# Attention, expert MLP and soft mixture on one core: scores on four array tiles, dummy products near the end, and a new order

## The chip, the cores and the metric

The kernel runs on one core of one Trainium2 chip. The metric is the device time of one execution in microseconds (us). The profile and the traces come from one further execution, recorded by the hardware profiler.

## The reference

Three stages follow each other. Everything is float32.

```
# 4 batches x 8 heads x 768 steps, head size 40: a gated recurrence
m_new  = max(f + m, i);  f' = exp(f + m - m_new);  i' = exp(i - m_new)
C = f' C + i' v k^T;     n = f' n + i' k
y = sigmoid(o) * (C q) / max(|n.q|, 1)
# y -> x: 3072 tokens x 320
h = x @ w_in (320 x 2048);  x = (h * sigmoid(h)) @ w_out (2048 x 320)
# soft mixture: 8 experts, 4 slots each
logits = x @ phi (320 x 32)
slot_in = softmax over tokens(logits)^T @ x
slot_out[e] = relu(slot_in[e] @ w1[e] (320 x 1024)) @ w2[e] (1024 x 320)
out = softmax over slots(logits) @ slot_out
```

## The kernel before, in words

**Attention** goes in 24 tiles of 128 steps (4 batches of 6), each with all 8 heads as 4 pairs. For a tile n, `load_qk` and `load_v` bring queries, keys and values; `mask`, `arg` and `exp` make the decay factors (`exp` on ACT, L566); `sc` multiplies keys with queries, per head and per half of 64 steps (L597); `sw` multiplies the scores with the factors (DVE, L604); `st` makes the state update (L629) and `sadd` adds it; `pv` takes scores and state to the values (L655); `xT` transposes the result and splits it into a high and a low part.

**The MLP** goes in 12 blocks of 256 tokens. `mlp.b.q` is one of 8 chunks of block b: 16 products of 128x256 (L702) and the activation (ACT, L704). `gU` transposes the activated rows (DVE, L711). `w_out` is not multiplied token by token: `wpT` and `wp` (L450 to L475) form `w_out @ phi` once, `lg` uses it for the logits of a block (L721), `lsum` and `slots` keep the running softmax and the weighted sums over tokens (L731, L745, L749, L762, L765). Before `wp`, each of the 16 pieces of `w_out` is loaded (L423) into one of five `cv` buffers and turned from its stored form into float32 by three operations, on ACT, DVE and DVE (L372, L374, L376).

**The end** begins after `slots.11`, the last block's sums: `slot_in` (L863, L873, L885), the experts' first layer `s1` (L905), its transposes (L915), the second layer `s2` in two column halves of 152 and 168 (L932), and `out` (L950), which multiplies with the softmax over slots and stores. The expert weights are loaded by `load_w1` and `load_w2` (L838 to L845). The 32 pieces of `w2` lie in memory that belongs to the MLP's buffers until these are done.

**What sets the order.** `ORDER` is a list of tokens written out by hand; a token such as `sc.7` runs the function `op_sc` for tile 7 to its next `yield`. The list's order is the order on each engine. The table `ENG` says for some operations whether DVE (V), ACT (A) or GpSimd (G, called POOL in the profile) does them. SP issues all DMAs, in order, with 8 in flight: each waits for the one eight before it.

**PSUM.** The accumulator memory is used through three tags, `h`, `t` and `w`, with two buffers each. A `w` buffer has two banks. Before the change `sc` writes into a `t` buffer of one bank, and `st` and `pv` write into a `w` buffer; `slots` takes both `w` buffers.

In the score product of the old kernel a head that lies on the upper 64 rows of the array writes to the upper 64 columns, and one on the lower rows to the lower columns: `tile_position=(o, o)`. `pv` uses all four combinations of row and column half, with a bank for each row half: `tile_position=(o, 64 * ch)`.

Of the kernel before, what the change touches and what calls it, by code (L numbers as in the profile page):

```python
# [1033 lines left out]
```

## Time and profile before

| what | value |
|---|---|
| time, median of 3 runs (range) | 458.77 us (457.52 to 459.79) |
| the profiled execution: time, span | 461.74 us, 459.8 us |
| granted TensorE clock, mean | 0.962 |
| busy: PE, weight loads, DVE, ACT, POOL | 408.9, 332.2, 268.8, 257.8, 114.5 us |
| share of the chain that ended last: PE, DMA, ACT, DVE | 50%, 16%, 13%, 12% |
| moved by DMA | 72.31 MB |

PE is TensorE's matrix products, PEld its weight loads, which run beside them. A granted clock of 1.0 is 2.4 GHz and 0.5 is 1.2 GHz. The chain is followed back from the last instruction, at each step to what released it. In a table of stretches each row has the length of the stretch, the busy time of each engine with the number of instructions, the clock, the mean busy share of the DMA engines (it can pass 1 for short stretches), and the transfer rate. In a timeline a row is a run of like instructions: start, duration, engine, line, and in brackets the idle time before it and what ended it.

### The profile page before, as it was taken

How to read it: one execution, taken by the hardware profiler on the slowest of the kernel's cores; microseconds unless marked ns; L12 is line 12 of the kernel's file. 1: busy time of each engine (PE TensorE's matmuls, PEld its weight loads, DVE VectorE, ACT ScalarE, POOL GpSimd, SP SyncE). 2: the span in 40 equal slices, each digit the busy share in tenths (PEclk: the TensorE clock that was granted, in tenths of full speed). 3: DMA queues.
4: the chain of work that ended last, by engine and by line, in shares of the span. 5: the costliest groups of instructions: out<-in, count | busy, mean ns of one | idle time of the engine just before them, and what ended most of it. 6: DMA issues, size and time to landing. Idle time of an engine off the chain costs nothing.

```text
span 459.8 us, 15017 instructions
## 1 busy us (share of the span) xinstructions
PE 408.9 (89%) x6458; PEld 332.2 (72%) x6458; DVE 268.8 (58%) x637; ACT 257.8 (56%) x473; POOL 114.5 (25%) x155
## 2 busy tenths in 40 slices
...
DMA packets 59218, 73.27 MB, mean 159 GB/s; under 512 B 4976, under 2 KB 46640, under 8 KB 59152
## 3 DMA queue, kind: packets, MB, share of 16 engines
q1 hardware_dynamic: 59152, 72.31, 53.9%
q8 instruction: 51, 0.84, 0.8%
q14 instruction: 15, 0.12, 0.1%
...
## 4 chain that ended last, share of the span: by engine, by line
PE 50%; DMA 16%; ACT 13%; DVE 12%; issue 4%; SPq 2%; POOL 1%; ACTq 0%; DVEq 0%; POOLq 0%
PE h L702 26%; DMA w<-in_moe_w 7%; PE w L655 4%; PE t L721 4%; PE w L762 3%; PE t L597 3%; DMA mb<-md 3%; ACT L704 3%; PE w L629 2%; DMA cv<-in_moe_w_out 2%; DMA rawi<-in_moe_w_in 2%; ACT gT L704 2%; ACT L745 2%; DMA vb<-in_vh 1%; PE t L675 1%
## 5 line engine op out<-in xcount | busy, mean ns | idle before, releaser
L702 PE MATMUL h<-xh,wh 128*128 128x256 f32 x384 | 85.7, 305 | 8.4 <-ACT gT L704 8.3
L704 ACT ACTIVATE gT<-h 128x512 f32<-128x512 f32 x96 | 55.5, 597 | 55.0 <-PE h L702 54.4
L702 PEld LDWEIGHTS h<-xh,wh 128*128 128x128 f32 x384 | 60.1, 193 | 25.4 <-ACT gT L704 17.6
L702 PE MATMUL h<-xl,wh 128*128 128x256 f32 x384 | 78.2, 286 | 0.0
L702 PE MATMUL h<-xh,wl 128*128 128x256 f32 x384 | 78.1, 285 | 0.0
L711 DVE STREAM_TRANSPOSE g<-gT 128x512 f32<-128x512 f32 x96 | 62.6, 685 | 3.0 <-ACT gT L704 2.8
L702 PEld LDWEIGHTS h<-xl,wh 128*128 128x128 f32 x384 | 60.4, 193 | 0.2 <-DVE xl L683 0.2
L702 PEld LDWEIGHTS h<-xh,wl 128*128 128x128 f32 x384 | 60.5, 194 | 0.0
L702 PE MATMUL h<-xh,wr 128*128 128x256 f32 x192 | 54.7, 285 | 0.0
L702 PE MATMUL h<-xl,wr 128*128 128x256 f32 x192 | 54.5, 284 | 0.0
L704 ACT ACT_TABLE_LOAD x36 | 46.2, 1283 | 7.9 <-DVE g L711 6.5
L765 DVE SCALAR_TENSOR_TENSOR acc<-acc,bm,w 128x512 f32<-128x512 f32 x48 | 33.2, 739 | 19.0 <-PE w L762 18.9
L702 PEld LDWEIGHTS h<-xh,wr 128*128 128x128 f32 x192 | 37.3, 194 | 0.0
L702 PEld LDWEIGHTS h<-xl,wr 128*128 128x128 f32 x192 | 37.2, 194 | 0.0
L584 POOL TENSOR_TENSOR xq<-qk,qb 104x512 f32<-104x512 f32 x23 | 29.8, 1294 | 23.8 <-PE w L655 11.1
L762 PE MATMUL w<-g,et 32*32 32x512 f32 x768 | 28.6, 620 | 5.1 <-DVE et L749 4.5
L604 DVE TENSOR_TENSOR xs<-t,arg 128x512 f32<-128x512 f32 x24 | 16.5, 689 | 26.4 <-ACT arg L566 12.2
L597 PEld LDWEIGHTS t<-qk 40*64 40x64 f32 x768 | 25.3, 138 | 5.4 <-issue 3.2
L566 ACT ACT_TABLE_LOAD x19 | 24.4, 1283 | 7.9 <-DVE arg L561 3.9
L597 PE MATMUL t<-qk 40*64 40x64 f32 x768 | 28.6, 225 | 0.0
L655 PE MATMUL w<-vb,xq 40*64 40x41 f32 x768 | 25.3, 230 | 1.6 <-DVE vb L640 1.5
L561 POOL TENSOR_TENSOR arg<-mb,arg 128x512 f32<-128x512 f32 x14 | 18.1, 1294 | 32.5 <-DMA mb<-md 15.7
...
## 6 DMA issues: line engine op xcount, KB each, us to landing
...
```

What stands on the lines that cost most here:

```text
L561: eng(f"arg.{n}", "G" if n else "V").tensor_tensor(out=arg, in0=mb.rearrange("p r (c t) -> p r c t", c=2), in1=arg, op=ALU.add)
L566: A_.activation(out=d["arg"], in_=d["arg"], func=AF.Exp, scale=-1.0)
L584: eng(f"qs.{n}", "G").tensor_tensor(out=xq[LR], in0=qkt[n % 2][LR, 0], in1=st[n]["qb"][LR], op=ALU.mult)
L597: T_.matmul(sc[o:o + 64, p, ch], qkn[o:o + D, 1, p, t], qkn[o:o + D, 0, p, t], start=True, stop=True, tile_position=(o, o))
L604: V_.tensor_tensor(out=d["xs"], in0=d["sc"], in1=d["arg"], op=ALU.mult)
L655: T_.matmul(op[64 * ch:64 * ch + 64, NP * par + p], a, vv[r, 1 - k, ch, p], start=(k == 0), stop=(k == 1), tile_position=(o, 64 * ch))
L702: T_.matmul(hp[:, z], w, x, start=(y == 0), stop=(y == 7))
L704: A_.activation(out=gt[0][:, 2 * q:2 * q + 2], in_=hp, func=AF.Silu)
L711: V_.transpose(out=us[blk][a][:, :, 4 * q:4 * q + 4].rearrange("p b c f -> p c b f"), in_=gt[0][:, 4 * q:4 * q + 4, 128 * a:128 * a + 128] ...
L721: T_.matmul(lp[32 * j:32 * j + 32], wp[:, j, 32 * q:32 * q + 32], gt[0][:, 4 * q + j], start=(q == 0), stop=(q == 3), tile_position=(0, 32 ...
L762: T_.matmul(ap[g][32 * b:32 * b + 32], d["et"][p, 4 * a + b], u[p, b].rearrange("p c f -> p (c f)"), start=(a == 0), stop=(a == 1), tile_p ...
L765: V_.scalar_tensor_tensor(out=acc[:, g], in0=acc[:, g], scalar=d["bm"][:, 3:4], in1=ap[g], op0=ALU.mult, op1=ALU.add)
```

## The change

The queries and keys come in a tile of ten column blocks instead of eight: four of q, four of k in which pairs 2 and 3 have their two heads on opposite row halves, and a second copy of q for pairs 2 and 3, swapped the same way. The scores then use all four combinations of row half and column half, in two banks of a `w` buffer, and `sw` reads two banks. `op_heat` is new: two products of a constant with itself into a `t` buffer that nobody reads; eight such tokens stand in the new order, three around `slots.11` and five in the output phase. `ORDER` and `ENG` are new throughout. Line numbers after the change are larger by 6 from L517 on and by 10 after `op_sc` (L597 is L606 now, L604 is L614, L629 is L639, L655 is L665, L702 is L712, L762 is L772, L863 is L873, L932 is L942, L950 is L960; the dummy product is L520).

```diff
@@ ENG, ORDER: all rows are new; one of each
-    "arg.0": "V", "arg.1": "G", "arg.10": "G", "arg.11": "G", "arg.12": "V", "arg.13": "G", "arg.14": "V", "arg.15": "V", "arg.16": "V", "arg.17": "G",
+    "arg.0": "V", "arg.1": "V", "arg.10": "G", "arg.11": "V", "arg.12": "G", "arg.13": "V", "arg.14": "V", "arg.15": "V", "arg.16": "G", "arg.17": "G",
...
+heat.1 row.10 load_w2.4.2 lsum.11 lsum.11 lsum.11 load_w2.3.2 lsum.11 slots.11 load_w2.6.3 load_w2.7.3 slots.11 slots.11 load_w2.6.2 load_w2.7.2 load_w2.4.3
@@
-        qkt.append(at.tile([128, 2, NP, 128], F32, name=f"qk{j}"))
+        qkt.append(at.tile([128, 10, 128], F32, name=f"qk{j}"))
@@
+    def op_heat(x):
+        p = psum("t", [128, 512])
+        for y in range(2):
+            T_.matmul(p[:, 256 * y:256 * y + 256], con[:, 0:128], con[:, 0:256], start=True, stop=True)
+        yield
@@ op_qs
-        eng(f"qs.{n}", "G").tensor_tensor(out=xq[LR], in0=qkt[n % 2][LR, 0], in1=st[n]["qb"][LR], op=ALU.mult)
+        eng(f"qs.{n}", "G").tensor_tensor(out=xq[LR], in0=qkt[n % 2][LR, 0:4], in1=st[n]["qb"][LR], op=ALU.mult)
@@ op_sc
-        sc = psum("t", [128, NP, 2, 64])
-        for p in range(NP):
+        sc = psum("w", [128, 2, 512])
+        for x in range(2):
             for ch in range(2):
                 t = slice(64 * ch, 64 * ch + 64)
-                for par in range(2):
-                    o = 64 * par
-                    T_.matmul(sc[o:o + 64, p, ch], qkn[o:o + D, 1, p, t], qkn[o:o + D, 0, p, t], start=True, stop=True, tile_position=(o, o))
-        d["sc"] = sc
+                for y in range(2):
+                    p = x + 2 * y
+                    for z in range(2):
+                        o = 64 * (z ^ y)
+                        f = 128 * x + 64 * ch
+                        T_.matmul(sc[64 * z:64 * z + 64, y, f:f + 64], qkn[o:o + D, 4 + p, t], qkn[o:o + D, 8 * y + x, t], start=True, stop=True, tile_position=(o, 64 * z))
+        d["sc"] = sc[:, :, 0:256]
@@ op_sw
-        V_.tensor_tensor(out=d["xs"], in0=d["sc"], in1=d["arg"], op=ALU.mult)
+        h2 = lambda t: t.rearrange("x (y p) c t -> x y (p c t)", y=2)
+        V_.tensor_tensor(out=h2(d["xs"]), in0=d["sc"], in1=h2(d["arg"]), op=ALU.mult)
@@ laid_out
-    d["qk"] = np.stack([qT, kT], 3)
+    swap = lambda x: x[:, ::-1, :, 2:]
+    d["qk"] = np.concatenate([qT, kT[:, :, :, :2], swap(kT), swap(qT)], 3)
```

Three places show how the order moves. First the DMA queue of SP at the start of the program, before:

```order
L240 DMA gb<-in_f_gate 96x256
L241 DMA gb<-in_i_gate 96x256
L423 DMA cv<-in_moe_w_out 128x640 x3
L245 DMA con<-in_const 128x321
L246 DMA gb<-in_const 96x656
L423 DMA cv<-in_moe_w_out 128x640
L288 DMA md_77<-gb 96x256
L423 DMA cv<-in_moe_w_out 128x640 x2
L381 DMA rawi<-in_moe_w_in 128x2x1024
L523 DMA qk_97<-in_qk 40x1024 x2
```

and after, from the 22nd row of its list, behind all of `w_in` (L381, L403), both tiles' queries, keys and values, and the first masks:

```order
L354 DMA qd<-gb 96x256
L423 DMA cv<-in_moe_w_out 128x640 x2
L529 DMA qk_97<-in_qk 40x1280 x2
L550 DMA mb<-md 64x4x128 x2
L552 DMA qb<-qd 64x4x128 x2
L423 DMA cv<-in_moe_w_out 128x640
L541 DMA kv_98<-in_kv 128x648
L542 DMA vb_95<-in_vh 128x328
L423 DMA cv<-in_moe_w_out 128x640 x6
L250 DMA ph<-in_moe_phi 128x2x32
L252 DMA ph<-in_moe_phi 64x32 x2
L423 DMA cv<-in_moe_w_out 128x640 x7
```

`w_out` (`cv`, sixteen pieces) stood at the head of the queue, interleaved with `w_in` (`rawi`); it now stands behind `w_in`, in a run of its own.

Second, SP near the end, where the pieces of `w2` are loaded (`w2_e_k` is piece k of expert e). Before:

```order
L838 DMA w1_6_1_5750<-in_moe2_w1 128x1024 [waits DMAHW7_49,DVE_49,PE_49]
L841 DMA w1_6_2_5751<-in_moe2_w1 64x1024 [waits DMAHW0_49]
L841 DMA w1_6_2_5751<-in_moe2_w1 64x1024 [waits DMAHW1_49]
L845 DMA w2_2_3_5744<-in_moe2_w2 128x2x320 [waits DMAHW2_49,DVE_49,PE_49]
L845 DMA w2_2_1_5728<-in_moe2_w2 128x2x320 [waits DMAHW3_49]
L845 DMA w2_1_1_5727<-in_moe2_w2 128x2x320 [waits DMAHW4_49]
```

After:

```order
L855 DMA w2_2_3_5757<-in_moe2_w2 128x2x320 [waits DMAHW2_49,DVE_49,PE_49]
L855 DMA w2_7_0_5738<-in_moe2_w2 128x2x320 [waits DMAHW3_49,PE_49]
L855 DMA w2_3_3_5758<-in_moe2_w2 128x2x320 [waits DMAHW4_49]
L855 DMA w2_0_1_5739<-in_moe2_w2 128x2x320 [waits DMAHW5_49,PE_49]
L851 DMA w1_6_2_5764<-in_moe2_w1 64x1024 [waits DMAHW6_49]
L851 DMA w1_6_2_5764<-in_moe2_w1 64x1024 [waits DMAHW7_49]
L848 DMA w1_7_0_5765<-in_moe2_w1 128x1024 [waits DMAHW0_49,PE_49,Activation_49]
L848 DMA w1_7_1_5766<-in_moe2_w1 128x1024 [waits DMAHW1_49]
L855 DMA w2_5_1_5744<-in_moe2_w2 128x2x320 [waits DMAHW2_49,PE_49]
L855 DMA w2_4_1_5743<-in_moe2_w2 128x2x320 [waits DMAHW3_49]
L855 DMA w2_4_2_5751<-in_moe2_w2 128x2x320 [waits DVE_49,DMAHW4_49,PE_49,Activation_49]
L855 DMA w2_3_2_5750<-in_moe2_w2 128x2x320 [waits DMAHW5_49]
```

The semaphore waits resolve as follows. Before, `w2_2_3` waits until `slots.11` has read the first half of its rows, and all behind it wait too: 28 more pieces of `w2` and `w1_7`. After, `w2_2_3` waits for `slots.10`, and the first load that waits for `slots.11` is `w2_6_3`, which follows the last row shown; 19 pieces of `w2`, it included, are left for the time after `slots.11` begins. Both kernels have the same loads in all. The order of the chunks of block 11 is 0, 1, 4, 5, 7, 6, 3, 2 before and 0, 1, 2, 3, 4, 5, 7, 6 after.

Third, PE around `slots.11`, before:

```order
L721 MATMUL t<-gT,wp 32x256 x16
L799 MATMUL t<-con,rs_5823 128x128 x2
L731 MATMUL t<-ls,con 128x256
L762 MATMUL w<-g,et 32x512 x32
L863 MATMUL t<-con,acc 128x32 x16
L873 MATMUL t<-wo,sg 32x320 x16
```

and after:

```order
L731 MATMUL t<-gT,wp 32x256 x16
L741 MATMUL t<-ls,con 128x256
L520 MATMUL t<-con 128x256 x4
L772 MATMUL w<-g,et 32x512 x32
L520 MATMUL t<-con 128x256 x2
L873 MATMUL t<-con,acc 128x32 x16
L883 MATMUL t<-wo,sg 32x320 x16
```

`lg.11` (L721) and `lsum.11` (L731) are followed by `slots.11` (L762); the two dummy pairs L520 now stand between, and one more behind `slots.11`. The transposes of the softmax over slots (L799) went to another place.

## Rows read from the trace of the kernel before

**Rows 1.** Stretches: length, busy (count) by engine, clock, DMA share, GB/s.

```profile
0.00:46.00 46.00, 27.89 (x175) 17.80 (x176) 31.19 (x66) 24.19 (x41) 9.99 (x18) 0.96 0.83 264
...
90.40:403.00 312.60, 295.72 (x5004) 251.68 (x5000) 197.97 (x473) 198.42 (x361) 84.49 (x114) 0.99 0.43 119
403.00:440.50 37.50, 32.43 (x384) 18.63 (x384) 7.95 (x25) 5.22 (x20) 3.36 (x6) 0.82 0.84 283
```

**Rows 2.** Timeline of SP, the last loads of w_out: start, duration, queue, line.

```profile
42.50 3.15 SPq L423 DMA_DIRECT2D cv<-in_moe_w_out  x3
```

**Rows 3.** Timeline of PE, the last groups of wpT.

```profile
48.71 4.01 PE L450 MATMUL t<-con,wo 128*128 128x128 f32 x16
```

**Rows 4.** Pieces of the chain that ended last: mlp.1's first chunk, lsum.11's exponential.

```profile
90.44 2.10 PE h L702 x16
...
400.63 1.28 ACT L745
```

**Rows 5.** Groups by line in 0 to 90.4 us: busy, mean ns, idle.

```profile
L372 ACT ACTIVATE wo<-cv 128x320 f32<-128x320 f32 x16 | 7.9, 501 | 14.6 <-DMA cv<-in_moe_w_out 14.4
...
L374 DVE TENSOR_SCALAR cv<-cv 128x320 uint32<-128x320 uint32 x16 | 5.7, 364 | 9.6 <-DMA cv<-in_moe_w_out 9.6
...
L376 DVE SCALAR_TENSOR_TENSOR wo<-wo,cv 128x320 uint32<-128x320 uint32 x16 | 8.5, 548 | 1.1 <-ACT wo L372 0.6
```

**Rows 6.** Timeline of PE in the middle: pv, xT, st, sc, and the next chunk.

```profile
311.38 0.33 PE L655 MATMUL w<-vb,xs 64*64 64x41 f32 x8
...
312.21 0.31 PE L655 MATMUL w<-vb,xq 40*64 40x41 f32 x8
...
314.47 0.49 PE L675 MATMUL t<-con,xa 128*128 128x128 f32 x3
...
319.26 0.68 PE L629 MATMUL w<-vz,kv 64*64 64x41 f32 x32
319.75 1.14 PE L597 MATMUL t<-qk 40*64 40x64 f32 x32
320.82 0.50 PE L702 MATMUL h<-xh,wh 128*128 128x256 f32 x2
```

**Rows 7.** Groups by line, whole span: ACT's table loads of one line, and sw.

```profile
L704 ACT ACT_TABLE_LOAD x36 | 46.2, 1283 | 7.9 <-DVE g L711 6.5
...
L604 DVE TENSOR_TENSOR xs<-t,arg 128x512 f32<-128x512 f32 x24 | 16.5, 689 | 26.4 <-ACT arg L566 12.2
```

**Rows 8.** Timeline of PE around slots.11, and s2's first half.

```profile
398.65 0.70 PE L731 MATMUL t<-ls,con 128*128 128x256 f32 x2
403.03 3.22 PE L762 MATMUL w<-g,et 32*32 32x512 f32 x64 [3.67 <-DVE et L749]
407.12 7.04 PE L863 MATMUL t<-con,acc 128*128 128x32 f32 x32 [0.87 <-DVE acc L765]
...
429.58 0.43 PE L932 MATMUL t<-w,wo 128*32 128x152 f32 x4
...
440.55 0.56 PE L950 MATMUL t<-so,cT 128*128 128x152 f32 x3
```

**Rows 9.** SP's waits ahead of w2's loads: total, times, longest.

```profile
SPq L845 <- DVE g L711: 8.8, 1, 8.8
...
SPq L845 <- PE w L762: 6.9, 1, 6.9
```

**Rows 10.** Timeline of SP, the loads behind that wait.

```profile
404.35 2.43 SPq L845 DMA_DIRECT2D w<-in_moe_w  x4
```

**Rows 11.** Groups by line: PE's waits for w2.

```profile
L932 PE MATMUL t<-w,wo 128*32 128x152 f32 x128 | 6.0, 296 | 3.3 <-DMA w<-in_moe_w 3.3
```

**Rows 12.** Timeline of PE, two of its idle times.

```profile
189.42 0.80 PE L702 MATMUL h<-xh,wh 128*128 128x256 f32 x2 [1.87 <-ACT gT L704]
...
238.55 1.93 PE L721 MATMUL t<-gT,wp 128*32 128x256 f32 x32 [1.75 <-DVE xs L604]
```

**Rows 13.** The stretch behind the first of them, columns as in rows 1.

```profile
189.00:192.00 3.00, 2.58 (x12) 2.58 (x13) 1.88 (x4) 2.68 (x4) 2.76 (x6) 0.53 0.89 297
```

More of the change, by code (lines that the diff above doesn't have):

```diff
@@ new lines @@
+load_v.3 vw.3 st.3 rows.3 arg.3 wpT.9 sadd.3.0 sdec.3.1 sadd.3.1 qs.3 wp load_qk.4 sc.4 exp.3 sw.3 pv.2 pv.2 pv.3 mlp.0.3 gU.0.0 wp xT.2 xT.2 pv.3 pv.3 pv.3
+xT.2 load_v.4 wp mlp.0.5 mask.4 sdec.4.0 xT.3 xT.3 vw.4 st.4 wp mlp.0.5 lg.0 sadd.4.0 sdec.4.1 xT.3 mlp.1.0 load_qk.5 load_o.2 load_o.3 sig.3 sig.2 gU.0.1
+rows.4 arg.4 exp.4 load_v.5 vw.5 sadd.4.1 gU.0.2 gU.0.2 gU.0.3 sw.4 lg.0 mlp.1.3 mlp.1.0 lsum.0 gU.0.1 mlp.1.3 lsum.0 lsum.0 lsum.0 qs.4 pv.4 pv.4 st.5 mask.5
+sdec.6.0 sdec.5.0 sadd.5.0 mlp.1.4 row.0 row.0 mlp.1.4 load_v.6 vw.6 lsum.0 mlp.1.1 mlp.1.1 slots.0 pv.4 pv.4 xT.4 rows.5 arg.5 qs.5 slots.0 slots.0 slots.0
@@ new lines @@
+xT.4 exp.5 mlp.1.6 slots.0 slots.0 sc.5 sw.5 row.0 slots.0 xT.4 rows.8 gU.1.0 gU.1.0 mlp.1.6 mlp.1.2 mlp.1.2 load_qk.6 mlp.1.7 mask.6 pv.5 rows.6 qs.6 st.6
+arg.6 exp.6 mlp.1.7 mlp.1.5 pv.5 pv.5 pv.5 xT.5 xT.5 sc.6 load_qk.7 sadd.6.0 rows.7 mlp.1.5 lg.1 sw.6 pv.6 load_v.7 gU.1.3 gU.1.2 xT.5 load_o.4 pv.6 pv.6
+sdec.6.1 lg.1 lsum.1 lsum.1 lsum.1 mlp.2.0 mlp.2.0 lsum.1 gU.1.2 sadd.6.1 mask.7 arg.7 mlp.2.1 mlp.2.1 row.0 gU.1.1 lsum.1 mlp.2.5 mlp.2.5 gU.1.1 row.0 gU.1.3
+gU.2.0 row.0 slots.1 pv.6 xT.6 slots.1 slots.1 slots.1 slots.1 sdec.7.0 slots.1 mlp.2.4 mlp.2.4 exp.7 row.0 row.0 xT.6 mlp.2.7 sc.7 sw.7 vw.7 st.7 mlp.2.6
@@ new lines @@
+mask.10 slots.2 qs.9 mlp.3.1 mlp.3.1 sadd.9.0 row.2 sdec.9.1 row.2 sig.5 arg.10 vw.10 exp.10 pv.9 pv.9 pv.9 pv.9 load_v.11 mlp.3.5 row.2 mlp.3.5 mlp.3.4
+slots.2 xT.9 gU.3.0 gU.3.0 sadd.9.1 load_qk.10 sc.10 sw.10 sdec.10.0 st.10 sadd.10.0 sdec.10.1 mlp.3.4 lg.3 xT.9 xT.9 mlp.4.2 mlp.4.0 gU.3.1 vw.11 sadd.10.1
+sdec.11.0 gU.3.2 qs.10 gU.3.1 mlp.4.2 lg.3 mlp.4.0 lsum.3 gU.3.2 row.2 row.2 st.11 sadd.11.0 lsum.3 lsum.3 row.2 gU.3.3 lsum.3 mask.11 rows.11 arg.11 exp.11
+pv.10 pv.10 load_qk.11 sc.11 mlp.4.3 mlp.4.3 sw.11 lsum.3 mlp.4.1 mlp.4.1 row.2 row.2 row.3 row.3 load_qk.12 row.3 slots.3 gU.3.3 mlp.4.6 slots.3 slots.3
@@ new lines @@
+slots.4 mlp.5.3 mlp.5.3 row.4 arg.13 exp.13 slots.4 slots.4 slots.4 mlp.5.1 mlp.5.1 sc.13 load_qk.15 vw.13 st.13 row.4 sw.13 mlp.5.0 mlp.5.0 sdec.13.0
+sadd.13.0 sdec.13.1 pv.13 mlp.5.7 mlp.5.6 mask.14 arg.14 row.4 pv.13 pv.13 pv.13 xT.13 gU.5.0 gU.5.0 gU.5.1 load_v.15 qs.14 vw.14 sadd.13.1 sc.14 exp.14
+sdec.14.0 gU.5.2 sw.14 st.14 sadd.14.0 mlp.5.6 mlp.5.7 load_o.7 sig.7 gU.5.3 lg.5 lg.5 pv.14 load_v.16 sdec.14.1 sadd.14.1 lsum.5 gU.5.3 xT.13 xT.13 mlp.6.0
+mlp.6.0 lsum.5 lsum.5 pv.14 lsum.5 mlp.6.4 mlp.6.2 mask.15 rows.15 arg.15 exp.15 gU.5.1 pv.14 load_o.8 lsum.5 slots.5 pv.14 xT.14 gU.5.2 slots.5 mlp.6.2 qs.15
```

115 lines of the change are left out of this document (49 added, 66 removed), and 46 rows, old and new, of the table ENG.

## The prediction, on record before the result was known

> **What bounds the kernel now.** I read the stretches first, then the timelines of PE and of SP, then the waits. In the long middle, 90.4 to 403 us, PE is busy for 295.7 of 312.6 us and DMA works at a share of 0.43 [rows 1]: there PE's own work sets the time, and a gain must come out of PE's products or out of its idle 17 us. The two ends are different. In the first 46 us DMA has a share of 0.83 at 264 GB/s and PE is busy for 27.9 us: the start waits for data. The last pieces of `w_out` are issued from 42.50 us on [rows 2]; wpT follows them at 48.71 [rows 3], and block 1's MLP begins at 90.44 [rows 4]. In the stretch from `slots.11` (403 us) to the end of the first half of `s2` (440.5 us) DMA has a share of 0.84 again, and the granted clock is 0.82, so part of it ran at 1.2 GHz [rows 1]. So I go by three places: the start up to mlp.1, the middle, and the end from `slots.11` on.
>
> **The start.** At the start of mlp.1, right behind lg.0, both orders have done the same PE work (tiles up to sc.4 and st.4, pv.0 to pv.3, mlp.0, wpT, wp, lg.0), so this point can be compared. Before, `w_out` heads the queue, and all eight chunks of mlp.0 come after wpT and wp. Now `w_in` and the tiles' data come first, `w_out` last, and seven of the eight chunks stand ahead of the last wpT groups: the MLP runs while `w_out` lands. By the shapes, the queue has to move this up to its last `w_out` piece: gates 192 KB, w_in 5120, constants 406, masks and their copies 384, q and k 1200, kv and values 1464, output gates 320, mb and qb 1024, w_out 5120, phi 48, together 15,278 KB or 15.64 MB. At the 264 GB/s of the first 46 us that is 59.2 us. The last piece is converted in 0.50 + 0.36 + 0.55 = 1.4 us [rows 5].
>
> What PE has left then I take from the old stretch between wpT and mlp.1, 90.44 - 48.71 = 41.7 us, which holds the same work and some that now comes earlier. Seven chunks of 2.10 [rows 4] leave it: 14.7. Of the five groups of wpT in it, 1.0 each by the row's 4.01 for four [rows 3], three leave: 3.0. Two scores (320.82 - 319.75 = 1.07 each), two states (0.49), one pv (0.95: eight runs at 0.118) and two transposes (0.5) leave [rows 6]: 5.1. The two scores that stay are cheaper by 0.5 each (below): 1.0. So 41.7 - 14.7 - 3.0 - 5.1 - 1.0 = 17.9 us stay, and mlp.1 begins at 59.2 + 1.4 + 17.9 = 78.5. **That is 12 us earlier.** Ends: if the queue is blocked by the five `cv` buffers, which must be converted before they are loaded again, nothing is gained (0); if the rest of PE's queue is mostly done in the waits, 20. I stay near the lower rate: the two groups on DVE, 0.91 us a piece, are faster than a piece lands (328 KB at 264 GB/s, 1.24 us). The larger q/k tiles are in the sum; the longer clearing of their padding stands in the shadow of the first loads, worth 2 x 0.2 us if that cover were gone.
>
> **The middle: scores.** A score product has 16 matmuls, seen as 32 passes, 1.07 us or 33 ns a pass on two array tiles [rows 6]. On four tiles `pv` starts a pass every 0.83/56 = 14.8 ns and `st` takes 0.49 us for 32. The scores are 64 wide where these are 41, so I take 0.58 us, a saving of 0.49 a tile, with 0.42 and 0.54 as ends. 19 of the 24 tiles lie behind mlp.1: **-9.3 us**. The Trainium skill, "TensorE: Matmul & The Clock Gate", section "Wait — 56ns, not 53.3ns?", says that successive matmuls never start closer than about 25 ns however narrow they are; by that a score would take 0.80 us and the saving would be 5.1 us. The trace disagrees: 14.8 ns a pass on four tiles.
>
> **The middle: what the score's new place costs.** The product held a `t` buffer and now takes one of the two `w` buffers until `sw` has read it. `st`, `pv` and `slots` use the same two. `sw` lasts 0.69 us, and waited for `arg` in ACT for 12.2 us in nine of its 24 cases [rows 7]. If each of the 12 `slots`, which takes both buffers, waits for one `sw`, that is 8.3 us; where the order leaves other PE work between, it is nothing. I take 3 us, nearer to nothing, because the order mostly puts chunks of the MLP behind a score: **+3**.
>
> ACT's table loads fall from 73 to 57 by the list, 1.28 us each [rows 7]. Most lie beside PE's work, so I count none, with one exception. Ahead of `slots.11` PE idles for 3.67 us [rows 8] for a chain in which ACT loads a table at 400.63 [rows 4]; in the new list the exponentials of `row` come directly ahead of it and need the same table. **-1.3.** Up to -8 stays as an end for the rest. The new choice of engines (`ENG`) moves work between DVE and GpSimd, which are busy for 198.0 and 84.5 of the 312.6 us; PE's queue covers it, or if that cover is gone it is a wait like those above. Middle: -9.3 + 3 - 1.3 = **-7.6 us**.
>
> **The end.** SP stood still ahead of `w2_2_3`, 8.8 us for a `g` tile and then 6.9 us for `slots.11` [rows 9], and went on at 404.35 [rows 10] with 29 pieces of `w2`. `s2` began at 429.58 [rows 8] and PE waited 3.3 us for data in it [rows 11]. Now 13 pieces go earlier and 19, 6.2 MB, remain: at this stretch's 283 GB/s 22 us, about when `s2` begins. **-3.3.** The stretch ran at a mean clock of 0.82 because PE fell to 1.2 GHz at 404.2 us, after the 3.67 us of idling: (1 - 0.82) x 37.5 = 6.75 us. Now two dummy pairs of 0.7 us (as L731's pair of passes) follow `lsum.11` at once; with the table load gone the idle time is 3.67 - 1.28 - 1.3, about 1.1 us. An idle time of 1.87 was followed by 0.53 [rows 12, 13], one of 1.75 was not followed by a fall; 1.1 lies below both, so I take the clock to hold. **-6.75.** The five pairs in the output phase come to 3.5 us, mostly in waits for copies; I take **+1**, with 0 and 3.5 as ends. The third pair, behind `slots.11`, lies in the 0.87 us in which PE waits for `acc`. End: **-9.1 us**.
>
> **Sum:** -12 - 7.6 - 9.1 = -28.7 us. The profiled execution took 461.7, so it would be 433; it lies 3 us above the median of 458.8, and against that the forecast is **430 us**.
>
> **The rivals.**
> *The clock falls all the same.* For it: PE is idle before the first product after the dummies, and there is the wait ahead of L863. Against: the idle times compared above. Then 6.75 us are lost again: 437.
> *Four tiles do not run side by side.* The score's operands fill 40 of 64 rows, and each bank takes products from both row halves. If a pass keeps its 33 ns, the 9.3 us are gone: 439. By the Trainium skill's 25 ns (same page and section) it would be 434; no row here shows such a floor.
> *The start gains nothing.* Five `cv` buffers and ACT, which must also activate mlp.0's chunks between the conversions, hold the queue back: 430 + 12 = 442. For it: SP waited for conversions before. Against: the landing is slower than the conversion. If the clock falls too, 449.
> *Fewer table loads help more,* by up to 8: 422.
> *Slower: the `w` buffers become the bound.* A score holds its buffer from its product until `sw`, which needs `exp` on ACT. Had all 24 the mean of the nine waits, 12.2/9 = 1.36 us, and then 0.69 of `sw`, and PE nothing to do meanwhile, 24 x 2.05 = 49 us come on in place of my 3: 476. It decides from 28.7 + 3 = 32 us on, 1.3 us a tile. The Trainium skill, "TensorEngine Tiling (Array Packing)", "Gotcha 1: PSUM Pressure", speaks for this rival: row tiles write to different banks and so need more PSUM; that two banks are taken where one was, the change itself shows. Against it: in the old trace PE idles 17 us in the whole middle with `st`, `pv` and `slots` in the same ring.
> *The change does not do what it says:* a dummy that delays `slots.11`. Two pairs cannot cost more than 1.4 us, which is inside the range.
>
> **How the numbers follow.** Forecast 0.50 (430; its own bounds 421 to 438); clock falls 0.13 (437); no side-by-side 0.05 (439); no gain at the start 0.12 (442); both 0.05 (449); table loads 0.08 (422); `w` buffers 0.07, half of it near no change or slower (476). The range takes the forecast's bounds and the one-sided cases up to 446, and at the low end the case of 422 with the start's better bound in part: 417. A measurement of this kernel tells 0.5%, 2.3 us, from no change. Faster 0.93, same 0.02, slower 0.05.
>
> **What would show it.** mlp.1 near 78 us, with seven chunks of mlp.0 ahead of the last wpT groups; runs of 32 score passes in 0.58 us; no wait of SP ahead of `w2_2_3` that lasts into `slots.11`; a clock of 1.0 from `slots.11` to `s2`, and no wait of `s2` for `w2`; and a middle, from mlp.1 to `slots.11`, of 305 us where it was 312.6. The prediction is wrong if mlp.1 begins later than 86 us, if PE's waits for `sw` sum to over 10 us, or if the clock is below 0.9 behind `slots.11`.

## The result, and the profile after

The changed kernel takes 428.72 us (median of 4 runs, 426.14 to 430.72), the kernel before 458.14 beside it: a ratio of 0.9357, 95% interval 0.9288 to 0.9427. The profiled execution is the slowest of the four, 430.72 us, with a span of 428.9 and a mean clock of 0.976. An execution more than 1.5% slower than the fastest of its kernel is left out of a ratio but not of a median; below this touches e3, e4 and e11. The forecast was 430, so the total came out; its terms did not. By the three places of the prediction, in us of the spans:

| stretch | before | after | predicted change | measured |
|---|---|---|---|---|
| start, up to mlp.1 | 90.4 | 85.8 | -12 | -4.6 |
| middle, mlp.1 to `slots.11` | 312.6 | 296.9 | -7.6 | -15.7 |
| `slots.11` to the end of `s2`'s first half | 37.5 | 27.5 | -10.05 | -10.0 |
| output phase, to the end of the span | 19.3 | 18.7 | +1 | -0.6 |
| sum | 459.8 | 428.9 | -28.7 | -30.9 |

The start gave 7 us less than forecast, the middle 8 more. First the stretches of the changed kernel, columns as in rows 1:

```profile
0.00:46.00 46.00, 28.57 (x362) 18.33 (x363) 30.19 (x60) 22.62 (x34) 15.24 (x20) 0.93 0.85 240
85.80:382.70 296.90, 286.38 (x5012) 243.37 (x5012) 207.03 (x488) 177.22 (x340) 80.84 (x112) 0.99 0.53 147
382.70:410.20 27.50, 26.31 (x389) 15.33 (x389) 8.09 (x26) 6.37 (x24) 2.37 (x2) 1.00 0.82 278
```

Beside [rows 1]: DMA carried 240 GB/s in the first 46 us, not 264. In the middle PE's busy time fell from 295.72 to 286.38 us and its idle time from 16.9 to 10.5. In the third stretch the clock is 1.00 where it was 0.82, and PE idles for 1.2 us instead of 5.1. This one execution was the best of its kind there: five others with the same dummies and the same early loads took 29.0 to 29.2 us (see the end of this document).

**The start.** The timeline of SP shows the last two runs of `w_out` loads (before: [rows 2]):

```profile
44.92 7.14 SPq L423 DMA_DIRECT2D cv<-in_moe_w_out  x6
...
55.54 6.95 SPq L423 DMA_DIRECT2D cv<-in_moe_w_out  x7
```

and SP's waits (total, times, longest) show what held them:

```profile
SPq L529 <- DVE qk L497: 10.5, 1, 10.5
...
SPq L423 <- DVE wo L376: 5.7, 4, 2.7
SPq L423 <- DVE cv L374: 5.3, 6, 1.8
```

The last piece is issued at 62.2 us and its conversion, which waits for it, begins at 66.68, by the timeline of DVE; the prediction had it landed at 59.2:

```profile
66.68 0.33 DVE L374 TENSOR_SCALAR cv<-cv 128x320 uint32<-128x320 uint32 x1 [0.53 <-DMA cv<-in_moe_w_out]
```

Two waits of these are the prediction's rival (the `cv` buffers, converted before they are loaded again: 5.7 + 5.3 us). One is new: the first q/k load waits 10.5 us until DVE has cleared the tile's padding (L497), which now stands behind conversions on DVE. I had costed that clearing at nothing. Then tile 3's q and k come late, as the chain that ended last shows:

```profile
63.42 7.03 DMA qk<-in_qk
70.50 1.12 PE w L606 x30
...
78.63 0.62 PE w L606 x32
...
85.79 4.02 PE h L712 x32
```

The last row is mlp.1 (before: [rows 4]). The score at 70.50 takes 1.12 us and a later one 0.62, because PE ran at 1.2 GHz for most of that stretch:

```profile
70.00:77.00 7.00, 6.50 (x82) 4.05 (x86) 3.44 (x9) 3.98 (x6) 1.48 (x3) 0.53 0.87 199
```

In the profiles of five kernels with this same start (this one and e2, e6, e7 and e11 below) mlp.1 begins at 85.8, 82.1, 84.3, 82.1 and 84.9 us, so the start alone is good for some 4 us between executions. In the two latest, this one and e11, the clock between 70 and 77 us is 0.53 and 0.55; in the other three it is 0.76 to 0.80.

**The middle.** The groups by line that answer to [rows 7], and the score's own (before, L597 was busy for 28.6 us in the same 768 passes):

```profile
L714 ACT ACT_TABLE_LOAD x28 | 35.9, 1283 | 1.6 <-PE h L712 1.1
...
L614 DVE TENSOR_TENSOR xs<-w,arg 128x512 f32<-128x512 f32 x24 | 16.4, 683 | 13.3 <-PE w L606 8.4
...
L606 PE MATMUL w<-qk 40*64 40x64 f32 x768 | 18.0, 227 | 3.0 <-DMA qk<-in_qk 2.1 <-DVE vb L650 0.8
```

Ahead of a product on the whole array a score takes 0.62 us instead of 1.07, which is 19 ns a pass. Ahead of a product on array tiles the next one starts 0.51 us after it (301.78 and 302.29 us on PE's timeline). `sw` (L614) waited mostly for `arg` before, and waits for the score now. The waits on PE and PEld for `sw` come to 1.4 us in all:

```profile
PE w L665 <- DVE xs L614: 0.4, 1, 0.4
...
PEld w L665 <- DVE xs L614: 1.0, 2, 0.6
```

The waits of the weight loads for the activations of the MLP (total, times, longest) were, before:

```profile
PEld h L702 <- ACT gT L704: 17.6, 16, 2.2
```

and are, after:

```profile
PEld h L712 <- ACT gT L714: 6.0, 7, 1.4
```

**The end.** PE around `slots.11` and `s2` (before: [rows 8]):

```profile
380.12 2.22 PE L520 MATMUL t<-con 128*128 128x256 f32 x8
382.67 2.35 PE L772 MATMUL w<-g,et 32*32 32x512 f32 x64 [0.34 <-DVE et L759]
...
403.76 1.32 PE L942 MATMUL t<-w,wo 128*32 128x168 f32 x32
...
405.60 4.66 PE L942 MATMUL t<-w,wo 128*32 128x168 f32 x128
410.19 0.57 PE L960 MATMUL h<-so,cT 128*128 128x168 f32 x3
```

`s2` (L942) waits for nothing. Two dummy tokens take 2.22 us, not 1.4, and leave 0.34 us of idling. SP no longer stands until `slots.11` (before: [rows 9, 10]):

```profile
363.62 4.30 SPq L855 DMA_DIRECT2D w<-in_moe_w  x4
...
371.48 2.85 SPq L855 DMA_DIRECT2D w<-in_moe_w  x4
```

### The profile page after: what moved, and what is told of

Read it like the earlier page. It is cut to its first block, busy times and chain, and to the rows that moved or that the text cites. A ratio compares the mean times of both kernels' runs of the same rounds, so it can differ in the third digit from the quotient of the medians.

```text
span 428.9 us, 15067 instructions
## 1 busy us (share of the span) xinstructions
PE 393.1 (92%) x6490; PEld 319.9 (75%) x6490; DVE 279.8 (65%) x648; ACT 236.1 (55%) x454; POOL 109.1 (25%) x147
## 4 chain that ended last, share of the span: by engine, by line
PE 66%; DVE 11%; issue 7%; DMA 6%; ACT 3%; POOL 2%; SPq 1%; DVEq 0%; POOLq 0%; ACTq 0%
PE h L712 31%; PE w L665 5%; PE w L772 5%; PE t L731 4%; PE w L606 3%; DMA qk<-in_qk 3%; PE w L639 2%; PE t L942 2%; DMA mb<-md 2%; PE h L915 2%; PE t L394 2%; PE t L685 2%; PE t L520 1%; PE t L741 1%; DVE g L721 1%
## 5 line engine op out<-in xcount | busy, mean ns | idle before, releaser
L712 PE MATMUL h<-xh,wh 128*128 128x256 f32 x384 | 85.1, 304 | 1.6 <-issue 1.4
L712 PE MATMUL h<-xl,wh 128*128 128x256 f32 x384 | 78.1, 285 | 0.4 <-DVE xl L693 0.4
L712 PE MATMUL h<-xh,wl 128*128 128x256 f32 x384 | 77.8, 284 | 0.0
L712 PEld LDWEIGHTS h<-xh,wh 128*128 128x128 f32 x384 | 60.3, 193 | 19.3 <-ACT gT L714 6.0
L721 DVE STREAM_TRANSPOSE g<-gT 128x512 f32<-128x512 f32 x96 | 63.8, 689 | 9.0 <-ACT gT L714 8.9
L712 PEld LDWEIGHTS h<-xl,wh 128*128 128x128 f32 x384 | 60.4, 193 | 0.6 <-DVE xl L693 0.6
L712 PEld LDWEIGHTS h<-xh,wl 128*128 128x128 f32 x384 | 60.3, 193 | 0.0
L712 PE MATMUL h<-xh,wr 128*128 128x256 f32 x192 | 54.5, 284 | 0.0
L712 PE MATMUL h<-xl,wr 128*128 128x256 f32 x192 | 54.4, 283 | 0.0
L775 DVE SCALAR_TENSOR_TENSOR acc<-acc,bm,w 128x512 f32<-128x512 f32 x48 | 33.4, 740 | 21.9 <-PE w L772 21.9
L712 PEld LDWEIGHTS h<-xl,wr 128*128 128x128 f32 x192 | 37.1, 193 | 0.0
L712 PEld LDWEIGHTS h<-xh,wr 128*128 128x128 f32 x192 | 37.0, 193 | 0.0
L772 PE MATMUL w<-g,et 32*32 32x512 f32 x768 | 28.0, 610 | 5.8 <-DVE et L759 4.0
L561 POOL TENSOR_TENSOR arg<-con,ahp 128x512 f32<-128x512 f32 x17 | 18.4, 1084 | 37.5 <-DVE xs L614 31.7
L665 PE MATMUL w<-vb,xs 64*64 64x41 f32 x768 | 25.2, 229 | 1.1 <-issue 0.7
L665 PEld LDWEIGHTS w<-vb,xs 64*64 64x64 f32 x768 | 20.9, 133 | 5.9 <-issue 2.5
L614 DVE TENSOR_TENSOR xs<-w,arg 128x512 f32<-128x512 f32 x24 | 16.4, 683 | 13.3 <-PE w L606 8.4
L590 POOL TENSOR_TENSOR xq<-qk,qb 104x512 f32<-104x512 f32 x16 | 20.9, 1304 | 15.2 <-DMA qb<-qd 7.9
L665 PE MATMUL w<-vb,xq 40*64 40x41 f32 x768 | 24.6, 227 | 0.0
L731 PE MATMUL t<-gT,wp 128*32 128x256 f32 x384 | 23.3, 382 | 0.0
```

What stands on the lines that cost most here:

```text
L561: eng(f"mask.{n}", "G").tensor_tensor(out=arg, in0=mk, in1=av.unsqueeze(3).to_broadcast([128, NP, 2, 64]), op=ALU.subtract)
L590: eng(f"qs.{n}", "G").tensor_tensor(out=xq[LR], in0=qkt[n % 2][LR, 0:4], in1=st[n]["qb"][LR], op=ALU.mult)
L614: V_.tensor_tensor(out=h2(d["xs"]), in0=d["sc"], in1=h2(d["arg"]), op=ALU.mult)
L665: T_.matmul(op[64 * ch:64 * ch + 64, NP * par + p], a, vv[r, 1 - k, ch, p], start=(k == 0), stop=(k == 1), tile_position=(o, 64 * ch))
L712: T_.matmul(hp[:, z], w, x, start=(y == 0), stop=(y == 7))
L721: V_.transpose(out=us[blk][a][:, :, 4 * q:4 * q + 4].rearrange("p b c f -> p c b f"), in_=gt[0][:, 4 * q:4 * q + 4, 128 * a:128 * a + 128] ...
```

## Experiments

The runs of one group shared the runs of the kernel before; its median was 458.76, 458.99 and 459.06 us in the three groups (and 459.22 for the last run). Against the changed kernel itself there is one yardstick: run again, unchanged, it gave 430.89 (e11), so medians that lie within some 2 us of 428.7 to 430.9 are not told apart. Its profiled execution also shows how much a stretch varies: the middle took 293.0 us in it and 296.9 in the first.

### The end: the clock or the data?

**e2_no_heat** leaves out the eight dummy tokens.

```diff
-load_w1.7 lsum.11 heat.6 slots.10 slots.10
+load_w1.7 lsum.11 slots.10 slots.10
...
-gU.11.3 load_w2.4.1 heat.1 row.10 load_w2.4.2
+gU.11.3 load_w2.4.1 row.10 load_w2.4.2
...
```

> The changed kernel without its eight dummy tokens. PE is then idle for about 2.4 us ahead of slots.11. Theory (the dummies keep the clock up): the clock falls to 1.2 GHz behind slots.11 for 10 to 14 us, 5 to 7 us are lost, time 434 to 436 us. Rival (the removed table load already makes the idle time short enough): the clock stays at 1.0 and the time is 427 to 429 us, a little less than with dummies because those of the output phase are gone.

431.81 us, ratio 0.9415 (0.9367 to 0.9463). `slots.11` on its timeline of PE:

```profile
376.53 3.35 PE L775 MATMUL w<-g,et 32*32 32x512 f32 x64 [2.39 <-DVE et L762]
```

and its stretches behind it:

```profile
376.00:384.00 8.00, 6.60 (x80) 4.18 (x80) 3.58 (x7) 0.17 (x1) 0.00 (x0) 0.58 1.05 368
384.00:392.00 8.00, 7.59 (x50) 4.97 (x50) 1.04 (x6) 1.44 (x6) 0.43 (x1) 0.57 1.07 363
```

PE idles for 2.39 us, 1.28 less than before the change, and runs at 1.2 GHz for most of the next 16 us. `slots.11` to the end of `s2`'s first half is 33.1 us. The output phase is 19.0 us (428.6 - 409.65) without its five dummies and 18.7 with them, so my +1 for them was nothing.

**e5_before_heat** puts two dummy tokens into the kernel before, at the same place.

```diff
+    def op_heat(x):
+        p = psum("t", [128, 512])
+        for y in range(2):
+            T_.matmul(p[:, 256 * y:256 * y + 256], con[:, 0:128], con[:, 0:256], start=True, stop=True)
+        yield
@@ ORDER, behind the first lsum.11
-lsum.11 lsum.11
+lsum.11 heat.6 heat.1 lsum.11
```

> The kernel before with two of the dummy tokens (two pairs of products) between lsum.11 and slots.11, nothing else. Its chain there still holds a table load, so of the 3.67 us of idle time some 2.4 us are left behind the dummies. Theory (that is as long as the 2.39 us behind which the clock fell in the run without dummies; dummies and the removed table load are both needed): the clock falls again, 457 to 461 us. Rival (the dummies alone keep the clock): it stays at 1.0 behind slots.11 and the time is 451 to 454 us.

459.00 us, ratio 1.0015 (0.998 to 1.005): no change. Its stretches from `slots.11` on, with the idle times of PE in `s2` (L941) behind them:

```profile
399.00:407.00 8.00, 4.97 (x86) 3.36 (x87) 3.74 (x8) 2.11 (x9) 0.00 (x0) 1.00 0.48 142
407.00:415.00 8.00, 7.17 (x60) 3.72 (x63) 2.82 (x12) 1.57 (x7) 3.12 (x6) 0.79 1.04 377
```

In `s2`:

```profile
426.52 0.45 PE L941 MATMUL t<-w,wo 128*32 128x152 f32 x2 [2.54 <-DMA w<-in_moe_w]
...
431.90 5.33 PE L941 MATMUL t<-w,wo 128*32 128x152 f32 x104 [2.07 <-DMA w<-in_moe_w]
```

The clock is 1.00 behind `slots.11` and 0.79 after. So neither expectation came true: the fall comes later and is shorter, and yet the time stays. PE begins `s2` 22.95 us behind the start of `slots.11` instead of 26.55 and waits there for `w2`: 2.54 + 2.07 us and more.

**e7_late_w2** is the other half: the changed kernel with one load that waits for `slots.11` put where it stands in the kernel before, ahead of the others.

```diff
-slots.10 load_w2.2.3 mlp.11.5
+slots.10 load_w2.6.3 load_w2.2.3 mlp.11.5
@@
-slots.11 load_w2.6.3 load_w2.7.3
+slots.11 load_w2.7.3
```

> The changed kernel with the one load that waits for slots.11 (w2_6_3) put where w2_2_3 stood, so that SP stands still there until slots.11, with 27 pieces of w2 and three of w1 behind it, as in the kernel before. Theory (with the clock at 1.0 PE reaches s2 before the data): the last piece lands some 35 us behind slots.11, the first half of s2 ends there instead of at 27.5 us, 435 to 438 us. Rival (the transfers are hidden all the same): below 431 us.

436.47 us, ratio 0.9488 (0.9434 to 0.9541). SP stands from 363.4 to 378.8 us, and PE pays behind it. First the timeline of SP:

```profile
363.03 0.34 SPq L852 DMA_DIRECT2D w<-in_moe_w  x1
378.82 2.42 SPq L859 DMA_DIRECT2D w<-in_moe_w  x5
```

then that of PE:

```profile
377.50 2.35 PE L776 MATMUL w<-g,et 32*32 32x512 f32 x64 [0.34 <-DVE et L763]
...
407.71 1.90 PE L946 MATMUL t<-w,wo 128*32 128x168 f32 x20 [4.84 <-DMA w<-in_moe_w]
```

The dummies and the clock behind them are as in the changed kernel, up to the wait for `w2`, and the stretch takes 38.3 us. Put together, in us from `slots.11` to the end of `s2`'s first half of one profiled execution each:

| | `w2` late | `w2` early |
|---|---|---|
| no dummies | 37.5 (before) | 33.1 (e2) |
| dummies | 37.1 (e5), 38.3 (e7) | 27.5 (changed); 29.0 to 29.2 (e1, e3, e6, e8, e11) |

The dummies are worth 0.4 us while `w2` is late, and about 4 us of the stretch once it is early (5.6 in the first profile). Of the timed medians that is 0.9 to 3.1 us, by the two runs of the changed kernel, and the intervals of the ratios overlap, so the gain is shown in the traces and not in the time. The early loads are worth 4.4 without the dummies and 9 to 11 with them, and here the time shows it: 436.47 in e7 against 428.72 and 430.89. My sum of two separate terms, 3.3 and 6.75, had the shape wrong: PE has to be fast and the data has to be there.

### The middle: tiles, buffers or table loads?

**e3_two_tiles** keeps the new order and both banks but puts each score back on two array tiles.

```diff
-                        o = 64 * (z ^ y)
+                        o = 64 * z
...
-                        T_.matmul(sc[64 * z:64 * z + 64, y, f:f + 64], qkn[o:o + D, 4 + p, t], qkn[o:o + D, 8 * y + x, t], start=True, stop=True, tile_position=(o, 64 * z))
+                        T_.matmul(sc[o:o + 64, y, f:f + 64], qkn[o:o + D, 4 + p, t], qkn[o:o + D, p, t], start=True, stop=True, tile_position=(o, o))
...
-    d["qk"] = np.concatenate([qT, kT[:, :, :, :2], swap(kT), swap(qT)], 3)
+    d["qk"] = np.concatenate([qT, kT, swap(qT)], 3)
```

> The changed kernel with its order, buffers and transfers, but each score product again on two array tiles (row half and column half the same). Theory (a score takes 1.07 us instead of 0.62 on an engine that is nearly always busy): 24 x 0.45 = 10.8 us more, time 437 to 440 us. Rival (PE has some 10 us of idle time behind mlp.1 in which this disappears): under 5 us more, time below 434 us.

436.66 us, ratio 0.9508 (0.9459 to 0.9557). The score's group by line:

```profile
L606 PE MATMUL w<-qk 40*64 40x64 f32 x768 | 29.7, 225 | 3.9 <-DMA qk<-in_qk 3.7 <-DVE xq L590 0.2
```

The middle:

```profile
83.40:387.50 304.10, 294.97 (x5012) 251.41 (x5008) 206.43 (x488) 179.24 (x342) 80.69 (x112) 0.99 0.52 143
```

The scores cost 29.7 us instead of 18.0, and the middle takes 304.1 us instead of 296.9 (293.0 in e11). PE is busy for 8.6 us more there, so most of the tiles' saving comes through: 6 to 8 us of the time, where 437 to 440 us was expected. The Trainium skill ("TensorE: Matmul & The Clock Gate", section "Wait — 56ns, not 53.3ns?") has a floor of about 25 ns from one start to the next; at 19 ns a pass on four tiles these runs disagree with it, as `pv` did.

**e4_before_four** puts the new score into the old order, with the few tokens moved that two `w` buffers demand, and without dummies.

```diff
@@ ORDER and ENG of the kernel before, with the changed functions
-arg.5 exp.5 sc.5 sw.5 slots.0
+arg.5 exp.5 slots.0
...
+slots.0 slots.0 sc.5 sw.5 slots.0
...
-lsum.3 lsum.3 load_v.11 sdec.10.1 sadd.10.1 sdec.11.0
+gU.3.1 lg.3 sdec.10.1 sadd.10.1 pv.10
```

Like tile 5's, the scores of tiles 11, 15 and 23 come later, and like tile 10's the state updates of nine tiles come earlier.

> The kernel before with its table and order, but with the score product, the tile of queries and keys and the w buffer of the change; 20-odd tokens of tiles 3, 5, 9 to 16, 18, 20 and 23 moved because the new use of the w buffers admits no other order. Theory (the score's saving comes whole and the ring of w buffers costs little): 24 x 0.45 = 10.8 us less and up to 5 us of waits more, time 447 to 453 us. Rival (waits for the w buffers eat the saving in an order that was not made for them): 455 to 465 us.

479.61 us, ratio 1.0364 (1.027 to 1.0458): slower than before. Where PE waits, by the group of `slots` by line:

```profile
L775 PE MATMUL w<-g,et 32*32 32x512 f32 x768 | 34.4, 670 | 14.9 <-DVE xs L617 10.0 <-DVE et L762 4.3 <-DVE g L724 0.6
```

and by the timeline of PE:

```profile
156.83 2.01 PE L775 MATMUL w<-g,et 32*32 32x512 f32 x28 [4.67 <-DVE xs L617]
...
341.22 2.01 PE L775 MATMUL w<-g,et 32*32 32x512 f32 x28 [3.24 <-DVE xs L617]
```

`slots` (L775) needs both `w` buffers, and one is a score's until `sw` (L617) has read it. This is the rival that I priced at 476 if the order left PE nothing to do meanwhile. It is real, and the order decides: the changed kernel has 1.4 us of such waits in all, none of them ahead of `slots`. The page "TensorEngine Tiling (Array Packing)" of the Trainium skill warns under "Gotcha 1: PSUM Pressure" that row tiling takes more PSUM; this run agrees, with 10.0 us of waits for `xs` ahead of `slots`. (That different row tiles write to different banks, as this page of the Trainium skill has it, is not so in this kernel: each of its two banks takes products of both row halves.) By the ratio the kernel is 17 us slower. The profiled execution, 472.81 us and the fastest of its four, is 11 us above that of the kernel before although its scores are busy for 11.5 us less (17.1 against 28.6), so the 10.0 us are not the whole loss. The mean clock is 0.944 here and 0.962 before, and which of these causes the other was not tried.

**e6_tables** gives the changed kernel 12 more table loads, by an exponential of one column ahead of some of the MLP's activations.

```diff
+        if q == 2 and 1 <= blk <= 8:
+            if "xt" not in sm:
+                sm["xt"] = cp.tile([128, 1], F32, tag="xt", name="xt", bufs=1)
+            A_.activation(out=sm["xt"], in_=con[:, 0:1], func=AF.Exp)
```

> The changed kernel with an exponential of one column ahead of one activation in each of blocks 1 to 8, so that ACT loads 69 tables instead of 57. Theory (fewer table loads are what shortened PE's idle time between mlp.1 and slots.11 from 16.9 to 10.5 us): PE waits longer for gT, 4 to 7 us more, 433 to 436 us. Rival (the loads are hidden behind PE's queue, and the idle time went for another reason): within 1.5 us of the changed kernel, 427 to 430 us.

428.88 us, ratio 0.9325 (0.9263 to 0.9386): nothing, with 34 + 6 loads at the two lines of the MLP where there were 28. So loads at these places cost nothing, and fewer loads as such are hardly what shortened the idle time of the middle. What is left is the order (the chunks, scores and products that stand between an activation and the product that waits for it) and the new choice of engines, `ENG`. No run takes these two apart, so this cause is argued and not shown.

### The start: what holds it?

**e1_pad_first** puts the clearing of the padding at the front of the order, ahead of DVE's conversions.

```diff
-arg.0 exp.0 pad load_qk.0 qb0
+arg.0 exp.0 load_qk.0 qb0
@@ at the front of ORDER
-init load_f scan
+pad init load_f scan
```

> The changed kernel with one token moved: the clearing of the query and key tiles comes first on DVE. In the changed kernel SP waited 10.5 us for that clearing (DVE L497, 18.39 to 20.85 us) and mlp.1 began at 85.8 us. Theory (that wait held back the queue and so w_out and mlp.1): mlp.1 begins 4 to 7 us earlier, time 422 to 425 us. Rival (the queue is paced by the five cv buffers and the transfer rate, and the standing queue was covered by w_in still landing): mlp.1 stays within 1.5 us, time 427 to 430 us.

427.45 us, ratio 0.9315 (0.9255 to 0.9374). mlp.1 begins at 81.7, but at 82.1 in e2 and e7, which have the old start; SP is through with `w_out` at 60.8 us, by its timeline:

```profile
52.79 8.04 SPq L427 DMA_DIRECT2D cv<-in_moe_w_out  x7
```

That is 1.7 us sooner than in the changed kernel's first profile and no sooner than in e2, e7 and e11 (60.7, 60.3 and 60.5). The wait of 10.5 us is gone and the queue is not earlier: something else paces it.

**e8_combined** adds two things to e1: tile 3's q and k ahead of the last `w_out` pieces, and no dummies in the output phase.

```diff
-load_wo.15 wo.15 wo.5 wo.15 wo.15
+load_qk.3 load_wo.15 wo.15 wo.5 wo.15 wo.15
...
-heat.7
...
-heat.4
...
-heat.2
...
-heat.0 heat.3
...
-load_qk.3
```

> The changed kernel with the clearing first on DVE, the loads of tile 3's queries and keys ahead of the last three pieces of w_out and their companions, and without the five dummy tokens of the output phase. Theory (at the start PE waited for tile 3's queries and keys and fell to 1.2 GHz behind it): mlp.1 begins at 79 to 81 us without a fall, time 423 to 426 us. Rival (the loads only change places, w_out comes later by as much): 427 to 430 us.

427.80 us, ratio 0.9296 (0.924 to 0.9351), with mlp.1 at 82.5: no gain over e1. SP is now through with `w_out` at 63.9 us instead of 60.8, so the rival has it: the loads change places.

**e9_late_g** loads the last six pieces of `w_out` into two buffers of the `g` ring, free at that time, so that their loads wait for no conversion.

```diff
-        raws["o", i] = cvt([128, DM, 2], U32)
+        late = [13, 14, 12, 10, 11, 8]
+        if i in late:
+            k = late.index(i)
+            if k % 3 == 0:
+                raws["gl"] = mp.tile([128, 3, DM, 2], U32, tag="g", name="late", bufs=GB)
+            raws["o", i] = raws["gl"][:, k % 3]
+        else:
+            raws["o", i] = cvt([128, DM, 2], U32)
```

> The changed kernel with the last six pieces of w_out loaded into two free buffers of the MLP instead of the five cv buffers, so that their loads wait for no conversion. SP waited 11 us for conversions ahead of w_out's loads, and DMA worked at a share of 0.64 to 0.73 from 48 to 60 us. Theory (the five buffers are what kept w_out from landing at 59 us): its last load is issued 3 to 6 us earlier than at 62.5 us, mlp.1 begins at 79 to 81 us, time 424 to 426.5 us. Rival (PE's own work or the transfer rate set mlp.1 by then): mlp.1 at 82 to 86 us as in the runs with this start so far, time 427 to 430 us.

Its timeline of SP at the start:

```profile
53.68 2.80 SPq L430 DMA_DIRECT2D late<-in_moe_w_out  x6
```

The queue is through at 56.5 us instead of 62.5, so the `cv` buffers did pace the issuing. In this run they did not pace the landing. The conversion of the last piece still waits for its data until 63.74 us, as in e2, where the `cv` buffers hold the queue; here is the timeline of DVE in e9 and then in e2:

```profile
63.74 0.33 DVE L374 TENSOR_SCALAR late<-late 128x320 uint32<-128x320 uint32 x1 [0.51 <-DMA late<-in_moe_w_out]
```

```profile
63.73 0.33 DVE L377 TENSOR_SCALAR cv<-cv 128x320 uint32<-128x320 uint32 x1 [0.64 <-DMA cv<-in_moe_w_out]
```

In e11 it is 64.03. SP's waits for conversions fell from 12.3 us in e2 to 4.3, and the data came no sooner. So the numbers of my theory for the start came true (mlp.1 at 80.1 instead of 85.7) and its mechanism did not: mlp.1 is 2 us earlier than in e2 and e7, and the clock between 70 and 77 us is 1.00 here and 0.76 and 0.80 there. The time, though, is 434.18 us, ratio 0.9455 (0.9414 to 0.9496). The stretch from `slots.11` on takes 38.2 us, as in e7, and SP stands still there again, by its timeline:

```profile
359.93 0.34 SPq L855 DMA_DIRECT2D w<-in_moe_w  x1
375.74 1.91 SPq L862 DMA_DIRECT2D w<-in_moe_w  x4
```

Two more buffers taken from the `g` ring shift which of its four block 11 gets. `w2` lies in the same memory, and the early piece `w2_2_3` now falls on a buffer that `slots.11` reads last.

**e10_late_g_pad** is e9 with e1's edit and without the output dummies.

> The same, with the clearing of the query and key tiles first on DVE as in e1 and without the five dummy tokens of the output phase. Theory (all that held the queue is taken away): mlp.1 at 78 to 80 us, time 422 to 425 us, faster than both kernels. Rival: as e9 or e1, 425 to 429 us.

435.73 us, ratio 0.9476 (0.9435 to 0.9517), with 38.1 us in the same stretch: the same. The last conversion of `w_out` ends at 62.7 us, 2.1 us earlier than in e1, and mlp.1 begins at 80.3.

**e11_again** is the changed kernel, as it is.

> The changed kernel itself, once more, on the chip of the two runs above. Theory (the fall of the clock at 70 to 77 us in its first profile is a matter of the single execution, since four other runs with the same start began mlp.1 at 82.1 to 84.3 us): mlp.1 begins 1.5 to 4 us earlier than at 85.7 us. Rival (it belongs to this kernel): 85 to 86.5 us. Time 427 to 430 us in both cases.

430.89 us, ratio 0.9369 (0.932 to 0.9419). Its profiled execution has mlp.1 at 84.9 and 29.1 us from `slots.11` on. The theory is wrong: mlp.1 is 0.8 us earlier and not 1.5 to 4, and the clock falls at the same place again, by its stretch:

```profile
70.00:77.00 7.00, 6.11 (x66) 2.71 (x68) 3.49 (x7) 5.00 (x7) 2.19 (x3) 0.55 0.61 153
```

**e12_late_g_swap** is e9 with four pieces of `w2` exchanged in memory, so that the early loads lie again in what `slots.10` frees.

```diff
+        for x, y in (((2, 3), (7, 2)), ((3, 3), (0, 3))):
+            w2t[x], w2t[y] = w2t[y], w2t[x]
```

> As e9 (the last six pieces of w_out land in the two free g buffers and their queue waits for no conversion), and now four pieces of w2 change places in memory: w2.2.3 with w2.7.2 and w2.3.3 with w2.0.3. In e9 the two extra buffers shift which of the four g buffers block 11 gets; the load of w2.2.3, early in SP's queue, then lies in a buffer that slots.11 reads last, and the queue stood there from 360 to 376 us. My theory: the gain of e9 at the start (mlp.1 at 80.1 us of the span instead of 85.7 and 84.9) is real, and its loss is the blocked queue alone. Then mlp.1 begins at 80 to 82, slots.11 to the end of s2's first half takes 27.5 to 30 us again instead of 38.2, and the time is 422 to 428 us. Rival 1: the time of the start is given back in the middle, as with e1: 427 to 431 with the short end. Rival 2: the end of e9 was slow for another reason (the clock, the lower data rate of an earlier slots.11): slots.11 to s2 stays near 38 us and the time near 434.

427.09 us, ratio 0.9291 (0.9233 to 0.9349), the lowest median of all, though not clear of the changed kernel's interval. The stretch from `slots.11` on is 30.8 us instead of 38.2, which misses the 27.5 to 30 of the theory by little: the blocked queue was most of the loss. By the timeline of SP it now goes on at 363.76 us:

```profile
363.76 2.85 SPq L864 DMA_DIRECT2D w<-in_moe_w  x4
```

mlp.1 on the timeline of PE:

```profile
80.48 0.50 PE L719 MATMUL h<-xh,wh 128*128 128x256 f32 x2
```

and the stretches from `slots.11` on:

```profile
376.00:384.00 8.00, 7.64 (x85) 6.08 (x74) 3.80 (x11) 0.63 (x3) 0.00 (x0) 0.82 0.99 327
384.00:392.00 8.00, 7.17 (x60) 2.73 (x56) 2.12 (x8) 2.19 (x10) 2.44 (x2) 0.75 1.07 369
```

The clock accounts for the 3.3 us between 30.8 and 27.5: (1 - 0.82) x 8 + (1 - 0.75) x 8 = 3.4. The earlier mlp.1 is kept (80.5, and a middle of 294.5), so rival 1 fails as a mechanism, though the time lies where both had it.

## Why the prediction was right, and where its terms were wrong

- **The start: the landing of `w_out` was put too early.** The -12 rested on "15.64 MB at the 264 GB/s of the first 46 us", all landed at 59.2. That step failed; the last piece is in at 66.7. The other terms held: the conversion takes 1.4 us and PE needs 17.6 from there to mlp.1, where I had 17.9. DMA was as busy as before in the first 46 us (0.85 against 0.83) but carried 240 GB/s; at that rate 15.64 MB take 65.2 us. Beside it stands the rival's mechanism, SP's 11 us of waits for `cv` buffers. The runs give it 0 to 2 us of the landing: e9 has 8 us less of such waits than e2 and lands at 63.7 like it, e10 is 2.1 us ahead of e1. In e9 DMA moved 16.5 MB by then (259 GB/s over 63.7 us), more than my 15.64: loads that stand behind `w_out` move beside it. Why the rate is lower in the new order, and why the first profile lands 3 us later than e2 and e11, stays open. The measured gain is 4.6 us in the first profile, 5.5 in the repeat and 8.3 in e2 and e7.
- **A fall of the clock at the start had no term.** At 0.53 from 70 to 77 us it costs (1 - 0.53) x 7 = 3.3 us of the 17.6, so that the 17.9 came out is partly luck.
- **The clearing of the padding was costed at nothing.** It made the first q/k load wait for 10.5 us. The cover held all the same: with the wait gone (e1) nothing is gained that can be told from no change.
- **The scores were right.** -9.3 was predicted. Behind mlp.1 the scores' own busy time fell by 8.2 us, from 22.0 to 13.8, and two tiles in the same order (e3) give back 8.6. A score is 0.51 or 0.62 us, by what follows it, where I had 0.58. That PE's busy time in the middle fell by just 9.3 is chance, since 2.2 us of dummies came into it.
- **The new place of the scores: +3 was too much, and the idle time had no term.** The waits for `sw` are 1.4 us where the old order had 1.75 in one case alone [rows 12], so the `w` buffers cost nothing that shows in this order; in the old order they help to make the kernel 17 us slower (e4). PE's idle time fell by 6.4 us, of which 2.2 are filled by dummies. The waits for the MLP's activations fell from 17.6 to 6.0 us; I had left whatever idle time the table loads might give back at an end of the range, -8. The idle time went, but not by the loads as such (e6).
- **The table load ahead of `slots.11` was right.** -1.3 was predicted; without dummies (e2) PE idles there for 2.39 us instead of 3.67.
- **The end was right in size by luck.** -10.05 was predicted for the stretch and -10.0 measured in the first profile; in five others it is -8.3 to -8.5, because the clock is 0.94 there. So the rival that the clock falls all the same comes true in part: (1 - 0.94) x 29.1 = 1.7 us of the 6.75. The idle time ahead of `slots.11` is 0.34 us where I had 1.1: a token is four passes, so 1.1 us where I had 0.7, and what stays is smaller. The two terms do not add up as I had them: alone they are worth 4.4 and 0.4 us, together 8 to 10.
- **The output phase** was +1 and is -0.6.

So the forecast of 430 hit by two errors that cancel, 7 us too much at the start and 8 too little in the middle. The range did its work, since each error stood in it as a rival of its own.
